# Local attention outputs from the third batch on: probabilities stationary, values moving, rows through DRAM into x by DMA transposes

## The chip, the cores and the metric

One core of a Trainium2 chip runs the whole kernel. The metric is the device time of one execution in microseconds (us), lower is better; the number for a kernel is the median of several executions. One further execution was taken with the hardware profiler, and every duration below comes from that one.

## What is computed

The reference is an attention with two fixed masks, followed by a bilinear feed-forward layer:

```python
# q, k, v: 8 batches, 8 heads, 576 positions, 64 features
rel = pos[:, None] - pos[None, :]
mask_local   = (rel >= 0) & (rel < 32)                                  # heads 0 to 3
mask_strided = (rel >= 0) & (pos[None, :] % 32 == pos[:, None] % 32)    # heads 4 to 7
attn = softmax(where(mask, q @ k.T / 8, -1e9));  o = attn @ v
x = o.transpose(0, 2, 1, 3).reshape(4608, 512)
out = ((x @ w_a) * (x @ w_b)) @ w_out       # w_a, w_b: 512 x 1536, w_out: 1536 x 512
```

Inputs and output are float32 in DRAM; the kernel calculates in bf16 with float32 sums.

## The kernel before, in words

**Two pipelines in one stream.** The feed-forward works on 9 tiles of 512 tokens. A tile `t` takes 16 slots, numbered `16t` to `16t+15`: 12 slots `ffn_ab` (one 128-wide piece of `d_ff` each: 4 matmuls with `w_a`, 4 with `w_b`, all 512 columns wide, written at L581; then a copy by ACT and a product by DVE), and 4 slots for the output. Tiles 2 to 8 (`FAST_Y`) take the output from seven half-size products (`y_plan`, and `y_tail` for the last tile) that are summed in a Strassen-like way; tiles 0 and 1 use `ffn_y` (L732).

The attention of batch `b` is cut into 8 units `u`, two for each pair of heads `c = u // 2`: units 0 to 3 are the local heads (3 blocks of 96 queries, each against 128 keys), units 4 to 7 the strided heads (4 blocks of 72). A step `S u` makes the scores on PE, `Exp` on ACT (L392) and the mask on DVE (L402), and leaves the probabilities in `p`, with keys on the partitions. A step `V u` multiplies them with the values. These steps are put between the slots by hand: `STEPS` for batches 1 and 2, `LATER` and `IN_Y` for the others, with positions counted from slot `16(b-1)`; `take(i)` runs those of slot `i`, and those of `i - 0.5` lie in the middle of the slot's matmuls. All five engines run in the order in which the program issues (a manual schedule); a tile framework adds the semaphores.

**The result x.** `xT` holds x transposed, 128 rows of features by 4 chunks (chunk `c` is the pair of heads `c`), in a ring of 4 batches. Tile `t` reads the end of batch `t-1` and the beginning of batch `t`, so batch `b` has to be in `xT` when slot `16b` starts. The first slot of a tile takes chunks 0, 1 and 2 first and chunk 3 last (for tile 1: chunk 1 last).

**The step V.** Two forms are in the kernel. For batches 0 and 1, `V_p` (L441) has the probabilities as weights (128 columns loaded) and 65 columns of values and ones moving; the result has queries on the partitions and the sum of the probabilities in column 65. `V_r` (L449) takes the reciprocal of the sums, `V_n` (L464) multiplies, and `step_X` (L510, L522) transposes on PE and copies into `xT`. From batch 2 on (`FIRST_D`), `step_VT` (L485) has the values as weights, with 64 columns of ones beside them, and 96 columns (strided: 72) of probabilities moving. The result is already transposed, and the sums stand in partitions 64 to 127. ACT makes the reciprocal as `Exp(-Ln(sum))` (L494, L495), and DVE multiplies straight into `xT`, one instruction for each head of the pair (L499 local, L501 strided).

**Loads.** K and Q of the batches from 2 on are loaded by GpSimd DMAs, transposed in blocks on DVE (`step_D`, L326 and L331), and put in place by DMAs on SP's queue (L341 for K, L345 for Q: ten for the local heads and ten for the strided heads of each batch). The local Q of batch `b` follows in slot `16(b-2)+9` (for batch 3: slot 27). The stores of the output stand on SP's queue too. SP issues in order, and in the built program each DMA also waits until the one eight places before it has landed.

**Tail.** `y_tail` makes the last tile's 14 products (seven kinds `k`, for even and odd rows `q`) in `TAIL_ORDER`. `y_post` moves each from PSUM (kinds 1, 7, 6, 5 and 3 by ACT, 4 and 2 by DVE; `+` is an addition on DVE), and `y_store` sends each finished part. The very last product, `21`, is made in two halves of 128 columns.

`fill_v` sets the columns of ones (64 to 127 of `vl` and `vs`) by GpSimd; `consts` has set column 64 alone already.

Of the kernel before, what the change touches and what calls it, by code (L numbers as in the profile page):

```python
# [8 lines left out]
BF16 = mybir.dt.bfloat16  # L9
# [5 lines left out]
FIRST_D = 2  # L15
RL = 6
RS = 8
# [4 lines left out]
LW = 96  # L22
# [8 lines left out]
def kernel(  # L31
# [10 lines left out]
    nc = tc.nc  # L42
    B, H, S, D = q.shape
# [9 lines left out]
    HL = H // 2  # L53
# [5 lines left out]
    sb = ctx.enter_context(tc.tile_pool(name="sb", bufs=3))  # L59
    fsb = ctx.enter_context(tc.tile_pool(name="ffn", bufs=2))  # L60
    pst = ctx.enter_context(tc.tile_pool(name="pst", bufs=1, space=bass.MemoryType.PSUM))
    dram = ctx.enter_context(tc.tile_pool(name="dram", bufs=2, space=bass.MemoryType.DRAM))
# [19 lines left out]
    vl_buf = [const.tile([128, HL * 6, VW], BF16, name=f"vl{i}") for i in range(2)]  # L82
# [30 lines left out]
    def zero_qz(i, eng, parts=((0, 0), (0, 1), (1, 0), (1, 1))):  # L113
        for j, z in parts:
            t = qz_buf[i][j][z]
            if (i, j, z) == (0, 0, 0):
                t = t[:, 1]
            if eng is nc.scalar:
                nc.scalar.copy(t, spare[:, :1].unsqueeze(2).to_broadcast(list(t.shape)))
            else:  # L120
                eng.memset(t, 0.0)
# [36 lines left out]
    XR = 4  # L158
    xT = const.tile([128, KD, XR * S], BF16)
# [11 lines left out]
    def fast_w(n, gs):  # L171
        a, b = ((wov[:, 0, 1], wov[:, 0, 0]), (wov[:, 1, 1], wf[:, 0]), (wov[:, 1, 1], wov[:, 0, 1]),
                (wov[:, 1, 0], wf[:, 1]))[n]
        nc.vector.tensor_tensor(wf[:, n, gs], a[:, gs], b[:, gs], op=ALU.subtract)
# [3 lines left out]
    def blocks(nm, z):  # L178
        z = int(z)
        return sb.tile([128, 2, (S, RS * GP)[z]], BF16, tag=f"t{nm}{z}", name=f"t{nm}{z}", bufs=1)  # L180
# [84 lines left out]
    def by_row(t):  # L265
        return t.rearrange("p (r h d) -> p h r d", h=2, d=D)

    def pair_up(nm, c):

        if (nm, c) == ("k", 1):  # L270
            t = shared[1][:96, -RL * 128:]
        else:
            t = blocks(*{"k0": "q0", "q0": "q1", "q1": "k0"}[f"{nm}{c}"])
            t = t.rearrange("p h n -> p (h n)")[:96, :RL * 128]
        nc.vector.tensor_copy(by_row(t), nats[1, nm, False][:, 2 * c:2 * c + 2])
        paired[1, nm, c] = t.rearrange("p (r m) -> p r m", r=RL)
# [85 lines left out]
    def unit(u):  # L362

        c, half = u // 2, u % 2
        return (c, half, 128, LW, 3) if c < 2 else (c, half, NP, NP, 4)
# [46 lines left out]
    xn = {}  # L412
# [33 lines left out]
    def V_r(b, u):  # L446
        c, half, M, n, G = unit(u)
        rc = sb.tile([128, 2, 4], F32, tag="rc", name="rc")
        nc.vector.reciprocal(rc[:n, :, :G].unsqueeze(3), held[b, "o", u][1])  # L449
        held[b, "rc", u] = rc  # L450

    def V_n(b, u):
        c, half, M, n, G = unit(u)
        ov, _ = held.pop((b, "o", u))
        rc = held.pop((b, "rc", u))
        if (b, c // 2) not in xn:
            x = sb.tile([128, RS * 4 * D], BF16, tag="xr", name="xr", bufs=2)
            xn[b, c // 2] = x[:n, :S // n * 4 * D].rearrange("p (g h d) -> p g h d", h=4, d=D)
        x = xn[b, c // 2][:, :, 2 * (c % 2):2 * (c % 2) + 2, :]
        if c < 2 or b >= FIRST_D:  # L460
            dst = x[:, G * half:G * half + G].rearrange("p g j d -> p j g d")
        else:
            dst = x[:, :, half, :].rearrange("p (g j) d -> p j g d", j=2)
        nc.vector.tensor_mul(dst, ov, rc[:n, :, :G].unsqueeze(3).to_broadcast([n, 2, G, D]))  # L464

    def step_V(b, u):
        if b >= FIRST_D:
            step_VT(b, u)
            return
        V_p(b, u)  # L470
        V_r(b, u)
        V_n(b, u)

    def step_VT(b, u):

# [48 lines left out]
    def step_X(b, c):  # L524
# [15 lines left out]
    STEPS = {1: {5.5: "Tk2", 6: "Tq2", 7: "S4 Tk3", 7.5: "S5", 8: "Tq3", 8.5: "V4", 9: "S6 V5 Pk0", 9.5: "S7 Pq0",  # L540
# [4 lines left out]
    LATER = {-1: "S0", 0: "S1", 1: "V0", 2: "S2", 3: "V1", 4: "S3", 5: "V2", 6: "S4", 7: "V3", 8: "S5", 9: "V4", 10: "S6",  # L545
             11: "V5"}
    IN_Y = {2: "S7", 6: "V6", 11: "V7"}
    FN = {"Tk": step_Tk, "Tq": step_Tq, "S": step_S, "V": step_V, "X": step_X, "W": lambda b, n: fast_w(n, slice(0, 3)),
          "s": S_px, "m": S_m, "L": lead_vl, "Pk": lambda b, c: pair_up("k", c), "Pq": lambda b, c: pair_up("q", c),
          "Z": lambda b, n: zero_qz(0, nc.vector, ((1, 1),)), "D": lambda b, n: step_D(FIRST_D, 0, "k", n)}  # L550

    def run(b, slot):
# [77 lines left out]
    def col(j):  # L630
        return slice(HN * j, HN * (j + 1))

    def y_store(eng, t, y, i, q, n=slice(0, d_model)):
        rows = out[TTOK * t:TTOK * (t + 1), n].rearrange("(a i s q) c -> a s i q c", i=2, s=8, q=2)
        eng.dma_start(out=rows[:, :, i, q], in_=y[i][:, q, n])
# [4 lines left out]
    def y_post(k, y, q, bank, n=slice(0, HN)):  # L640

        part = lambda i, j: y[i][:, q, HN * j:HN * (j + 1)]
        if k == "+":
            nc.vector.tensor_tensor(part(1, 1), part(1, 1), part(0, 1), op=ALU.add)
        elif k in "1765":
            nc.scalar.copy({"1": part(0, 0), "7": part(0, 1), "6": part(1, 0), "5": part(1, 1)}[k], bank)  # L646
        elif k == "4":
            nc.vector.tensor_tensor(part(1, 0), bank, part(1, 0), op=ALU.add)
        elif k == "2":
            nc.vector.tensor_tensor(y[0][:, q, n], bank, y[0][:, q, n], op=ALU.add)  # L650
        elif k == "3":
            nc.scalar.copy(part(0, 1), bank)

    Y_ORDER = [(x[0], int(x[1])) for x in "10 11 70 71 60 61 40 41 50 51 20 21 30 31".split()]
    TAIL_ORDER = [(x[0], int(x[1])) for x in "10 70 11 71 60 61 40 41 50 51 30 31 20 21".split()]

    def y_plan(t):

# [22 lines left out]
    def y_tail(t):  # L681

        plan, y = products(t), y_bufs()
        banks = [{x: mm_bank([128, HN]) for x in "ZXY"},
                 {"X": psum4["o"].tile([128, 2, 512], F32, tag="o", name="end")[:, 0, :HN],
                  "Z": pst.tile([128, 2, 512], F32, tag="st", name="end")[:, 0, :HN]}]
        for k, q in TAIL_ORDER:
            b, lhs, rhs = plan[k]
            cuts = [slice(0, HN)]
            if (q, k) == (1, "2"):  # L690
                cuts = [slice(0, 128), slice(128, HN)]
            for n in cuts:
                if (q, k) == (1, "2"):
                    bank = mm_bank([128, 128])
                else:
                    bank = banks[q][b]
                for g in range(FG):
                    nc.tensor.matmul(bank, lhsT=lhs(g, q), rhs=rhs(g)[:, n], start=g == 0 and k in "172",  # L698
                                     stop=g == FG - 1, skip_group_check=True)
                    if g < FG - 1:  # L700
                        yield y
                y_post(k, y, q, bank, n)
                if k == "5":
                    y_post("+", y, q, None)
                    y_store(nc.sync, t, y, 1, q)
                elif (q, k) == (0, "2"):
                    y_store(nc.sync, t, y, 0, q)
                elif (q, k) == (1, "3"):
                    y_store(nc.scalar, t, y, 0, q, col(1))
                elif (q, k) == (1, "2"):  # L710
                    y_store(nc.scalar if n.start == 0 else nc.sync, t, y, 0, q, n)
                yield y
# [48 lines left out]
    with tc.manual_schedule(engines={ENG.PE, ENG.SP, ENG.Pool, ENG.DVE, ENG.Activation}):  # L761
# [11 lines left out]
        for x, src in ((raw[0], k), (raw[1], q)):  # L773
            nc.sync.dma_start(out=x[:96].rearrange("p (h r d) -> p h r d", h=2, d=D),
                              in_=src[0, 0:2].rearrange("h (p r) d -> p h r d", r=RL))
# [16 lines left out]
        for nm in ORDER:  # L792
            if nm[0] == "*":
                spin(int(nm[1:]))
            elif nm == "C0":
                for x, cp, n in ((raw[0], nc.vector.tensor_copy, "k"), (raw[1], nc.scalar.copy, "q")):
                    t = nats[0, n, False][:, 0:2].rearrange("p h r d -> p (h r d)")
# [40 lines left out]
        for b in range(1, B):  # L838
            for pos, names in (STEPS.get(b) or {16 * (b - 1) + x: n for x, n in LATER.items()}).items():
                steps.setdefault(pos, []).append((b, names.split()))  # L840
# [6 lines left out]
        def do(i, fn, *args):  # L847
            at.setdefault(i, []).append(lambda: fn(*args))

        soon = {}  # L850
        for t in FAST_Y[:-1]:
            soon[16 * t + 10] = [lambda t=t: fast_s(t, 2, slice(4, 6))]
            soon[16 * t + 11] = [lambda t=t, n=n: fast_s(t, n, slice(4, 6)) for n in (0, 1)]
        do(0, fill_v, vl_buf[0])
        do(0, fill_v, vs_buf[0])
        for c in range(4):
            do(0, load_wo, c)
# [25 lines left out]
        for i, jz in ((2, (0, 0)), (3, (1, 0)), (0, (0, 1))):  # L883
            do(i, zero_qz, 0, nc.vector, (jz,))
        do(14, rezero, 1)
        do(27, fill_v, vl_buf[1])
        do(28, fill_v, vs_buf[1])
        for n, slot in enumerate((16, 16, 19, 20)):
            do(slot, fast_w, n, slice(3, 6))
# [50 lines left out]
```

## Time and profile before

| What | Value |
|---|---|
| Median of 3 runs | 328.97 us (328.81, 328.97, 331.59) |
| The profiled execution | 330.64 us, of which the program's span is 328.9 us |
| PE, busy share of the span | 322.3 us (98%) |
| DVE / ACT / POOL | 251.6 us (76%) / 210.2 us (64%) / 151.4 us (46%) |
| DMA engines, mean busy share | 90% or more in most slices up to 222 us, then falling |
| First matmul of tile 2 | at 94.28 us |

The span begins with the first instruction of the program; some 1.7 us of the profiled execution lie around it. "Busy" for PE means that some matmul was in the array; the ends of matmuls are modelled, so the distance between starts says more than a duration.

How to read the lines that follow. A group of instructions has its line, engine, operation, output and inputs, form and count, then "busy us, mean ns" and the idle time before. A timeline line has its start, its length, and how many instructions were merged into it (x6). SPq is the issuing of a DMA on SP's queue, and its length is that of the issuing, not of the transfer.

### The profile page before, as it was taken

How to read it: one execution, taken by the hardware profiler on the slowest of the kernel's cores; microseconds unless marked ns; L12 is line 12 of the kernel's file. 1: busy time of each engine (PE TensorE's matmuls, PEld its weight loads, DVE VectorE, ACT ScalarE, POOL GpSimd, SP SyncE). 2: the span in 40 equal slices, each digit the busy share in tenths (PEclk: the TensorE clock that was granted, in tenths of full speed). 3: DMA queues.
4: the chain of work that ended last, by engine and by line, in shares of the span. 5: the costliest groups of instructions: out<-in, count | busy, mean ns of one | idle time of the engine just before them, and what ended most of it. 6: DMA issues, size and time to landing. Idle time of an engine off the chain costs nothing.

```text
span 328.9 us, 7658 instructions
## 1 busy us (share of the span) xinstructions
PE 322.3 (98%) x2820; PEld 206.2 (63%) x2820; DVE 251.6 (76%) x529; ACT 210.2 (64%) x345; POOL 151.4 (46%) x280
## 2 busy tenths in 40 slices
PE   8899999999999999999999999999999999999994
PEld 6664555455555577557999885559555954584474
DVE  7747797888877998799879988898878745626642
ACT  6753766468778776877677767776777743323341
POOL 8845947689956644763565446634012001100000
PEclk9979999999999999999999999999999999999999
DMA  9999999799999599999799979797024040004004
GB/s 159 139 204 203 200 184 171 150 170 142 141 214 108 94 87 93 90 225 107 73 85 179 148 77 97 140 193 84 20 63 128 2 131 0 0 2 129 0 2 128
DMA packets 98725, 37.50 MB, mean 114 GB/s; under 512 B 76672, under 2 KB 95744, under 8 KB 98688
## 3 DMA queue, kind: packets, MB, share of 16 engines
q0 software_dynamic: 85968, 19.48, 63.8%
q1 hardware_dynamic: 12432, 17.34, 17.7%
q8 instruction: 22, 0.36, 0.5%
q10 hardware_dynamic: 288, 0.20, 0.2%
q14 instruction: 15, 0.12, 0.1%
HBM read 39.51 MB, written 9.44 MB: 149 GB/s over the span
## 4 chain that ended last, share of the span: by engine, by line
PE 93%; POOL 2%; DMA 2%; DVE 1%; ACT 0%; issue 0%; POOLq 0%
PE mm L581 55%; PE mm L669 17%; PE mm L732 6%; PE st L384 4%; PE o L485 4%; DMA tk<-in_v_dram 2%; PE mm L698 2%; PE ab L581 1%; POOL shared L196 1%; PE end L698 1%; PE o L441 1%; POOL vl L224 1%; PE tp L510 1%; PE tp L286 0%; PE tp L295 0%
## 5 line engine op out<-in xcount | busy, mean ns | idle before, releaser
L581 PE MATMUL mm<-xT,wa_sb 128*128 128x512 bf16 (+1 forms) x472 | 110.3, 357 | 0.0
L581 PE MATMUL mm<-xT,wb_sb 128*128 128x512 bf16 (+1 forms) x472 | 110.2, 357 | 0.0
L598 ACT COPY a_sb<-mm 128x512 f32<-128x512 f32 x106 | 62.1, 586 | 45.3 <-PE mm L581 44.5
L906 POOL CAST pace<-pf 1x1 f32<-1x1 bf16 x87 | 24.6, 283 | 113.6 <-DVE pf L601 109.8
L581 PEld LDWEIGHTS <-wb_sb 128*128 128x128 bf16 x480 | 46.6, 98 | 44.6 <-issue 1.1
L601 DVE TENSOR_TENSOR pf<-a_sb,mm 128x512 bf16<-128x512 f32 x84 | 57.1, 679 | 18.4 <-PE mm L581 14.2
L581 PEld LDWEIGHTS <-wa_sb 128*128 128x128 bf16 x480 | 42.7, 98 | 31.3
L392 ACT ACTIVATE p<-st 128x576 bf16<-128x576 f32 (+1 forms) x64 | 41.6, 650 | 6.7 <-PE st L384 6.1
L494 ACT ACTIVATE xr<-o 64x576 f32<-64x576 f32 x48 | 31.1, 648 | 22.6 <-PE o L485 22.3
L495 ACT ACTIVATE xr<-xr 64x576 f32<-64x576 f32 x48 | 32.8, 684 | 1.5
L499 DVE TENSOR_TENSOR xT<-o,xr 64x288 bf16<-64x288 f32 x48 | 21.6, 450 | 13.8 <-ACT xr L495 13.2
L501 DVE TENSOR_TENSOR xT<-o,xr 64x288 bf16<-64x288 f32 x48 | 21.4, 446 | 11.9 <-ACT xr L495 11.2
L669 PEld LDWEIGHTS <-ps 128*128 128x128 bf16 x288 | 27.9, 98 | 3.1
L646 ACT COPY y_sb<-mm 128x512 f32<-128x512 f32 (+1 forms) x28 | 15.6, 556 | 18.5 <-PE mm L669 13.0
L669 PE MATMUL mm<-wf,ps 128*128 128x256 bf16 x216 | 25.6, 273 | 0.0
L732 PE MATMUL mm<-wo_sb,pf 128*128 128x512 bf16 x96 | 23.4, 379 | 0.0
L242 POOL DMA_DIRECT2D vs<-in_v_dram x24 | 19.7, 820 | 4.9 <-PE mm L669 2.4
L669 PEld LDWEIGHTS <-pf 128*128 128x128 bf16 x216 | 20.3, 98 | 2.5 <-issue 0.2
L669 PE MATMUL mm<-wo_sb,pf 128*128 128x256 bf16 x144 | 18.5, 273 | 0.1
L211 POOL DMA_DIRECT2D ql<-in_q_dram x24 | 16.0, 666 | 5.0 <-DMA wo_sb<-in_moe_w_out_dram 3.8
L211 POOL DMA_DIRECT2D kl<-in_k_dram x24 | 16.0, 667 | 4.9 <-issue 3.2
L615 DVE TENSOR_TENSOR ps<-pf 128x512 bf16<-128x512 bf16 (+1 forms) x48 | 17.8, 380 | 0.5
(152 smaller groups left out, 471.3 us busy)
## 6 DMA issues: line engine op xcount, KB each, us to landing
out_dram<-y_sb SPq DMA_DIRECT2D x12, 512.0 KB, 4.9
out_dram<-y_sb SPq DMA_DIRECT2D x11, 256.0 KB, 3.0
vl<-in_v_dram POOLq DMA_DIRECT2D x6, 384.0 KB, 6.7
kl<-in_k_dram POOLq DMA_DIRECT2D x24, 72.0 KB, 3.2
ql<-in_q_dram POOLq DMA_DIRECT2D x24, 72.0 KB, 3.4
vs<-in_v_dram POOLq DMA_DIRECT2D x24, 72.0 KB, 3.8
wo_sb<-in_moe_w_out_dram POOLq DMA_DIRECT2D x4, 384.0 KB, 9.1
natk<-in_k_dram POOLq DMA_DIRECT2D x20, 72.0 KB, 3.2
```

What stands on the lines that cost most here:

```text
L211: nc.gpsimd.dma_start(out=t[32 * h:32 * h + 32], in_=src[b, h].rearrange("(i y) d -> y i d", y=32))
L392: nc.scalar.activation(p[:M, :, :W], st[:M, :, :W], ACT.Exp, scale=scale)
L494: nc.scalar.activation(r, sums, ACT.Ln)
L495: nc.scalar.activation(r, r, ACT.Exp, scale=-1.0)
L499: nc.vector.tensor_mul(dst[:, W * half:W * (half + 1)], o[:64, j, :W], r[:, j])
L501: nc.vector.tensor_mul(dst.rearrange("d (p r) -> d p r", r=RS)[:, :, G * half:G * (half + 1)], o[:64, j, :W].rearrange("d (g p) -> d p g", ...
L581: nc.tensor.matmul(ps_[:, c0:c0 + n], lhsT=w[:, kk, 128 * f:128 * (f + 1)], rhs=xT[:, kk, x0:x0 + n], start=(kk == first and c0 == 0), sto ...
L598: nc.scalar.copy(a_sb, ab[0])
L601: nc.vector.tensor_mul(pf[:, f, :].rearrange("p (i a s) -> p a i s", i=2, s=16), halves(a_sb), halves(ab[1]))
L669: nc.tensor.matmul(bank[b][:, q], lhsT=lhs(g, q), rhs=rhs(g), start=k in "172" and q == 0 and g == 0, stop=g == FG - 1, skip_group_check=True)
L732: nc.tensor.matmul(ybank[j], lhsT=pf[:, f, 128 * j:128 * (j + 1)], rhs=wo_sb[:, f], start=(f == 0), stop=(f == FD - 1))
L906: nc.gpsimd.tensor_copy(pace, done)
```

## The change

Units 0 to 3 of batches 2 to 7 (24 units) take the form with the probabilities as weights again: `V_p`, `V_r`, `V_n`, into a tile `xl` of which there is one. Once `V3` has filled it, `O0` writes it as rows to a DRAM tile (two of these), by one DMA on SP's queue: 96 partitions by 6 rows of 512 bytes. Then `I0` and `I1` read it back with two DMA transposes, also on SP's queue, 576 rows by 128 columns each, into chunks 0 and 1 of `xT`. For batch 2, `O0` stands in slot 26 and `I0 I1` in slot 28; for later batches in slots 7 and 9 after `16(b-1)`. Units 4 to 7 stay as they were. The fill of the ones beside the local values goes. The last tile's products come in another order, and two of its stores move.

```diff
         if (b, c // 2) not in xn:
-            x = sb.tile([128, RS * 4 * D], BF16, tag="xr", name="xr", bufs=2)
+            if b >= FIRST_D:
+                x = sb.tile([128, RL * 4 * D], BF16, tag="xl", name="xl", bufs=1)
+            else:
+                x = sb.tile([128, RS * 4 * D], BF16, tag="xr", name="xr", bufs=2)
...
     def step_V(b, u):
-        if b >= FIRST_D:
+        if b >= FIRST_D and u >= 4:
             step_VT(b, u)
             return
...
+    scratch = {}
+
+    def rows_out(b, _):
+
+        scratch[b] = dram.tile([S, HL * D], BF16, tag="xd", name="xd")
+        nc.sync.dma_start(out=scratch[b].rearrange("(g p) e -> p g e", p=LW),
+                          in_=xn.pop((b, 0)).rearrange("p g h d -> p g (h d)"))
+
+    def rows_in(b, c):
+
+        nc.sync.dma_start(out=xT[:, c, S * (b % XR):S * (b % XR + 1)], in_=scratch[b][:, 128 * c:128 * (c + 1)],
+                          transpose=True)
...
-             2: {20: "S0", 20.5: "S1", 21.5: "V0", 22: "S2", 23: "V1", 23.5: "S3", 24.5: "V2", 25: "S4", 26: "V3", 26.5: "S5",
-                 27.5: "V4", 28: "S6", 28.5: "V5", 29: "S7", 29.5: "V6", 30.5: "V7"}}
-    LATER = {-1: "S0", 0: "S1", 1: "V0", 2: "S2", 3: "V1", 4: "S3", 5: "V2", 6: "S4", 7: "V3", 8: "S5", 9: "V4", 10: "S6",
+             2: {20: "S0", 20.5: "S1", 21.5: "V0", 22: "S2", 23: "V1", 23.5: "S3", 24.5: "V2", 25: "S4", 26: "V3 O0", 26.5: "S5",
+                 27.5: "V4", 28: "S6 I0 I1", 28.5: "V5", 29: "S7", 29.5: "V6", 30.5: "V7"}}
+    LATER = {-1: "S0", 0: "S1", 1: "V0", 2: "S2", 3: "V1", 4: "S3", 5: "V2", 6: "S4", 7: "V3 O0", 8: "S5", 9: "V4 I0 I1", 10: "S6",
              11: "V5"}
...
-    TAIL_ORDER = [(x[0], int(x[1])) for x in "10 70 11 71 60 61 40 41 50 51 30 31 20 21".split()]
+    TAIL_ORDER = [(x[0], int(x[1])) for x in "10 70 60 11 40 50 71 30 61 20 51 41 31 21".split()]
...
                 if k == "5":
                     y_post("+", y, q, None)
+                if k == "54"[q]:
                     y_store(nc.sync, t, y, 1, q)
...
                 elif (q, k) == (1, "3"):
-                    y_store(nc.scalar, t, y, 0, q, col(1))
+                    y_store(nc.sync, t, y, 0, q, col(1))
...
-        do(0, fill_v, vl_buf[0])
         do(0, fill_v, vs_buf[0])
...
-        do(27, fill_v, vl_buf[1])
         do(28, fill_v, vs_buf[1])
```

More of the change, by code (lines that the diff above doesn't have):

```diff
@@ L548 @@
     FN = {"Tk": step_Tk, "Tq": step_Tq, "S": step_S, "V": step_V, "X": step_X, "W": lambda b, n: fast_w(n, slice(0, 3)),
-          "s": S_px, "m": S_m, "L": lead_vl, "Pk": lambda b, c: pair_up("k", c), "Pq": lambda b, c: pair_up("q", c),
+          "s": S_px, "m": S_m, "L": lead_vl, "O": rows_out, "I": rows_in, "Pk": lambda b, c: pair_up("k", c), "Pq": lambda b, c: pair_up("q", c),
           "Z": lambda b, n: zero_qz(0, nc.vector, ((1, 1),)), "D": lambda b, n: step_D(FIRST_D, 0, "k", n)}
```

## The prediction

> **What bounds the kernel.** I read the page first: the busy shares, the slices, the chain that ended last.
>
> ```profile
> PE 322.3 (98%) x2820; PEld 206.2 (63%) x2820; DVE 251.6 (76%) x529; ACT 210.2 (64%) x345; POOL 151.4 (46%) x280
> ...
> PEclk9979999999999999999999999999999999999999
> DMA  9999999799999599999799979797024040004004
> ...
> PE 93%; POOL 2%; DMA 2%; DVE 1%; ACT 0%; issue 0%; POOLq 0%
> ```
>
> PE is busy for all of the span but the ends, at the full granted clock from the fourth slice on, and 93% of the chain is PE. Busy alone proves little, so I compared the distances between matmul starts: those 512 wide stand 0.216 us apart throughout. After 22 us all gaps beyond such distances come to about 0.3 us. So an edit pays only by what it takes from PE's stream or from the tail, and every wait that reaches PE is paid in full. The DMA engines are 90% busy or more in most slices until 222 us.
>
> Next, the groups by shape, for what is exchanged:
>
> ```profile
> L495 ACT ACTIVATE xr<-xr 64x576 f32<-64x576 f32 x48 | 32.8, 684 | 1.5
> L494 ACT ACTIVATE xr<-o 64x576 f32<-64x576 f32 x48 | 31.1, 648 | 22.6 <-PE o L485 22.3
> ...
> L499 DVE TENSOR_TENSOR xT<-o,xr 64x288 bf16<-64x288 f32 x48 | 21.6, 450 | 13.8 <-ACT xr L495 13.2
> ...
> L485 PE MATMUL o<-p,vl 128*128 128x96 bf16 x144 | 10.0, 206 | 0.0
> ...
> L464 DVE TENSOR_TENSOR xr<-o,rc 96x384 bf16<-96x384 f32 x8 | 4.3, 547 | 0.2
> ...
> L441 PE MATMUL o<-vl,p 128*128 128x65 bf16 x48 | 2.6, 194 | 0.3 <-DMA vl<-in_v_dram 0.3
> ...
> L449 DVE RECIPROCAL rc<-o 96x6 f32<-96x6 f32 x8 | 1.5, 190 | 2.5 <-PE o L441 2.4
> ```
>
> The new form of a local unit runs here already, in batches 0 and 1 (L441, L449, L464), so it has prices. The durations of 206 and 194 ns hide the difference, since each includes the pipeline's end. The timeline of PE shows it, one unit of each form between its neighbours:
>
> ```profile
> 57.02 0.34 PE L441 MATMUL o<-vl,p 128*128 128x65 bf16 x6
> 57.20 0.60 PE L732 MATMUL mm<-wo_sb,pf 128*128 128x512 bf16 x2
> ```
>
> ```profile
> 200.56 0.42 PE L485 MATMUL o<-p,vl 128*128 128x96 bf16 x6
> 200.82 0.38 PE L581 MATMUL mm<-xT,wa_sb 128*128 128x512 bf16 x1
> ```
>
> From the unit's start to the next work's: 0.18 us with 65 columns moving, 0.255 us (unrounded) with 96.
>
> **PE's saving.** 24 units (6 batches by 4) times 0.075 us is 1.8 us, all of it on the path. Bounds: 1.7 to 1.9, the rounding of the two rows. Here a rule speaks against the change. The Trainium skill, "TensorE: Matmul & The Clock Gate", section "Back-to-back issue gap", has a sustained pair of weight load and matmul at about 81 ns for 128 columns, set by both; if the load of 128 weight columns set the pace, narrowing what moves would save nothing, and the sum would be 1.8 us worse. The rows disagree: the pairs stand 42.5 and 29.5 ns apart, in proportion to the columns.
>
> **ACT and DVE.** ACT loses 24 × (648 + 684) = 32 us. DVE exchanges 2 × 450 ns for 190 + 547 ns, 24 × 163 = 3.9 us less, and it no longer waits for ACT's two passes. I take nothing for either: the PE stream beside them has no stalls that a faster ACT or DVE could remove beyond the 0.3 us. The cover is PE's own work; it could be lost only if DVE became late, and it has less to do. The two fills on POOL (1.4 us each) go too, at nothing: POOL mostly waits for the pace of DVE.
>
> **The new path through SP.** O0 is a 288 KB write, I0 and I1 are 144 KB reads with transposition. I0 must wait until O0 has landed; for batches 3 to 7, SP's ten DMAs for the next batch's local Q and K are queued behind that wait, and S0 of the next batch, on PE, waits for those. The slack is long: the units V3 of batches 3 to 6 start at 109.89, 143.91, 178.10 and 212.46, the tiles that need them at 128.47, 162.50, 197.02 and 231.04, 18.6 to 18.9 us later. The chain between: 1.2 us on DVE; O0's issue and landing, at most 6.5 (the longest store's); two issues of 0.6; a landing of at most 5.9 (the longest on SP between 85 and 92 us): 14.8 us. SP is at its busiest for batch 6: two stores and two K blocks hold it until 216.3; then 6.5 + 1.2 + 5.9 ends at 229.9, still before 231.04. Next batch's Q: the DMAs that began at 220.03 there had landed for S0 by 224.46, and S0 starts at 230.5; with O0 landed at 219.3 (3 us) to 222.8 and two issues they begin 0.5 to 4 us later. Zero for all these; up to 1 us each if every bound meets.
>
> Batch 2 is different. There, Q of batch 3 goes to SP in slot 27, ahead of I0 and I1 in slot 28, and a store stands between:
>
> ```profile
> 85.14 0.54 SPq L345 DMA_DIRECT2D qz10l<-tq  x1
> ...
> 89.54 1.22 SPq L345 DMA_DIRECT2D qz11l<-tq  x1
> 90.80 0.60 SPq L345 DMA_DIRECT2D qz10l<-tq  x1
> 91.62 0.51 SPq L345 DMA_DIRECT2D qz11l<-tq  x1
> 92.23 1.50 SPq L743 DMA_DIRECT2D out_dram<-y_sb  x3
> ```
>
> ```profile
> 94.28 0.81 PE L581 MATMUL mm<-xT,wa_sb 128*128 128x512 bf16 x3
> ```
>
> The ten DMAs keep SP from 85.14 to 92.13, though the chunk that tile 2 takes first, at 94.28, now comes behind them. Worked forward: O0 goes out at about 82 (V3's matmuls at 79.85, reciprocal and product in DVE's order), before Q is ready, and has long landed. Batch 3's Q waits for a DVE transposition that ended at 85.11; in DVE's new order (each V 0.16 us shorter, no wait for Ln and Exp) I get 84.3. So the ten end between 90.6 (without the 1.22 us stall) and 92.1, the first store 0.6 later, I0 goes out between 91.2 and 92.8, I1 0.6 us after. I take I1 at 92.9. PE needs I1's chunk with tile 2's second matmul, at 94.50.
>
> How long a transposing DMA takes, no row shows. Nearest rows: on this queue from 85 us on, blocks of 36 to 40 KB land 1.8 to 5.9 us after issue, and the stores of 256 KB at 92 to 94 us in 2.3 to 3.5. I take 3.0, as the plain DMAs nearest in size and place. I1 then lands at 95.9, and PE stands for 1.4 us. Bounds: 91.8 + 1.8 = 93.6, no stall; 93.4 + 5.9 = 99.3, 4.8 us; with the 9.1 us that a 384 KB block of the third weight matrix takes on GpSimd's queue (the median there), 8.0 us.
>
> The skill has a price: "VectorE: DVE Perf Modes", section "The three transpose paths", gives 1309 ns for 128×128 through the DMA crossbar, which for 576 rows is 5.9 us in series (an estimate), 11.8 for both chunks, and would make the stall about 9 us and the time about 336; no row here shows it.
>
> **The tail.** The chain's end:
>
> ```profile
> 323.75 1.47 ACTq L635 DMA_DIRECT2D out_dram<-y_sb  x2
> 324.00 0.96 DVE L650 TENSOR_TENSOR y_sb<-mm,y_sb 128x256 f32<-128x256 f32 x3 [1.14 <-PE mm L698]
> 324.49 1.19 SPq L635 DMA_DIRECT2D out_dram<-y_sb  x2
> ```
>
> The last product is the same, so DVE ends at 324.97 as before. SP's last store went out at 325.12 because the one before it held SP until 325.03; in the new order that one (kind 3, ready after its copy at about 324.4) ends SP's issue at about the same time. What changes is traffic: the 256 KB of `20` leave some 2 us earlier, and 128 KB stand in front of the last 64 KB. Those took 2.72 us to land, the 128 KB store 2.52. I take 0.2 us gained; bounds −0.1 (PE may wait where `60` follows `10` with one product between; `30` after `50` does so before without a gap) and 0.4.
>
> **The sum.** The profiled execution took 330.64 us (span 328.9 and 1.7 around it): −1.8 − 0.2 + 1.4 is −0.6, or 330.0 on its scale. It lies 1.67 above the median, so on the median 328.97 − 0.6 = 328.4.
>
> **Rivals.** *In time:* I0 and I1 land by 94.5 (an SP queue without its 1.22 us stall, and a landing near 2.5 us). Then 328.97 − 2.0 = 327.0, between 326.7 and 327.4. For: DVE and ACT are relieved just there. Against: landings of 3.7 to 5.9 us on that queue between 85 and 90.
>
> *Slow transposes:* the crossing of a row-wise source into 128 partitions takes a good deal longer than a plain copy, or the SP queue spends more than 0.6 us to issue one. It decides at tile 2's first two matmuls, and makes the kernel slower by over 1% (332.3) from a stall of 5.3 us, I1 landing after 99.8. At 9.1 us from issue the stall is 7.5 and the time 334.5. A longer gap can also cost the clock: the page's slice with a clock of 7 is where matmuls of 512 stood twice as far apart after early gaps. For: nothing in the rows excludes it, and DMA engines are 90% busy there. Against: 256 KB stores land in 2.3 to 3.5.
>
> *No narrower in effect:* weight loads set the pace of the new units, PE saves nothing, 330.2 with the stall. The rows of batch 1 speak against it.
>
> **How the numbers follow.** Stall of 0.4 to 5.3 us at tile 2 (327.4 to 332.3): 0.39, forecast 328.4. In time: 0.24. Slow transposes: 0.28. No narrower: 0.03. A gain that I see no row for, below 325.7: 0.06. So faster by over 1% 0.06, within 1% 0.66, slower by over 1% 0.28; 1% is about what a measurement of this kernel can tell from no change. The range goes from 326.6, the lower end of "in time", to 334.5, leaving out half of "slow transposes" (0.14) and the 0.06 below.
>
> **What would show it.** In the profile after: the local units' starts 0.18 us apart from the next work; L494, L495 halved in count, L499 gone; the gap before tile 2's first or second matmul, near 94 us, against I0's and I1's landing; no gap at the starts of tiles 3 to 7, and none before S0 of batches 4 to 7; the last landing some 0.2 us sooner after PE's end. I am wrong if the landing of a transpose lies outside 1.8 to 5.9 us, if gaps appear at the later tiles (then SP's wait for O0, not batch 2's place in the queue, is what costs), or if PE's distances do not shrink.

## The result and the profile after

| | Before | After |
|---|---|---|
| Median | 328.99 us (4 executions, 328.81 to 331.59) | 333.0 us (4 executions, 332.53 to 334.68) |
| Ratio, 95% interval | | 1.0116, 1.0079 to 1.0153 |
| The profiled execution, its span | 330.64, 328.9 us | 334.68, 333.0 us |

The kernel became 4 us slower, where 0.6 us faster was forecast. A ratio leaves out executions that took over 1.5% more than the fastest of their kernel: in the experiments one of e2, three of e8, and one of the kernel before. First the page of the changed kernel, the lines that were shown of before:

```profile
PE 321.2 (96%) x2788; PEld 204.9 (62%) x2820; DVE 246.7 (74%) x529; ACT 178.8 (54%) x297; POOL 148.1 (44%) x278
...
PEclk9999999999978999999999999999999999999998
DMA  9999999999996897999999999999226030004004
...
PE 82%; DMA 5%; DVE 4%; POOL 3%; issue 2%; SPq 1%; ACT 1%; DVEq 0%; POOLq 0%
```

ACT's busy time fell by 31.4 us (32 had been worked out) and DVE's by 4.9 (3.9), and it bought nothing. (32 records of matmuls are missing from this trace: 2788 of 2820.) PE's share of the chain fell from 93% to 82%, and DMA's rose from 2% to 5%. The clock's row has a 7 and an 8 in the twelfth and thirteenth slices, from 91.6 to 108.2 us; before's 7 in the third slice, from 16 to 25 us, is gone. (The 8 in the last slice lies behind the last matmul.) So something happens around tile 2's start. The groups by shape and the timeline of PE say that the exchange itself came as planned:

```profile
L511 ACT ACTIVATE xr<-xr 64x576 f32<-64x576 f32 x24 | 16.4, 683 | 0.8
L510 ACT ACTIVATE xr<-o 64x576 f32<-64x576 f32 x24 | 15.6, 648 | 10.6 <-PE o L501 10.5
L467 DVE TENSOR_TENSOR xl<-o,rc 96x384 bf16<-96x384 f32 x24 | 13.3, 554 | 0.8
L441 PE MATMUL o<-vl,p 128*128 128x65 bf16 x192 | 10.9, 193 | 0.3
```

```profile
103.24 0.34 PE L441 MATMUL o<-vl,p 128*128 128x65 bf16 x6
103.42 0.81 PE L597 MATMUL mm<-xT,wa_sb 128*128 128x512 bf16 x3
```

A unit of the new form takes 0.18 us of PE's stream. Next, the timeline of PE where tile 2 begins (L597 is before's L581; brackets hold the idle time in front and what ended it):

```profile
95.96 0.59 PE L597 MATMUL mm<-xT,wa_sb 128*128 128x512 bf16 x1 [3.53 <-DMA xT<-xd]
97.32 0.59 PE L597 MATMUL mm<-xT,wa_sb 128*128 128x512 bf16 x1 [0.77 <-DMA xT<-xd]
98.12 1.49 PE L597 MATMUL mm<-xT,wb_sb 128*128 128x512 bf16 x3 [0.22 <-issue]
```

Without the wait the first of these matmuls would have begun at 92.27, right behind S0 of batch 3, and the second at 92.48. They began at 95.96 and 97.32, one for each transpose: a gap of 3.7 us and one of 1.1, together 4.8 by distances of starts. Then the clock, as busy times by stretch; the columns are the stretch, its length, PE's busy time (and matmuls), then PE's weight loads, DVE, ACT and POOL, and last the granted clock, the DMA share (the whole time of all packets begun in the stretch, so it can pass 1) and GB/s:

```profile
88.00:92.20 4.20, 4.20 (x32) 2.04 (x30) 2.19 (x4) 3.17 (x5) 1.91 (x4) 1.00 1.25 139
92.20:95.50 3.30, 0.23 (x6) 0.12 (x3) 2.07 (x4) 1.22 (x3) 1.49 (x3) 1.00 1.35 196
95.50:102.30 6.80, 5.35 (x17) 2.21 (x18) 1.32 (x3) 1.24 (x2) 0.42 (x2) 0.50 0.78 169
102.30:110.00 7.70, 7.65 (x56) 3.95 (x56) 6.03 (x12) 3.50 (x6) 5.35 (x11) 1.00 0.85 89
```

PE is idle in nearly all of the second stretch, and in the third, after the wait, it runs at half clock: the rows change at 95.47 and 102.29, two windows of 3.41 us, and matmuls of 512 columns start 0.43 us apart.

Why were the transposes late? The timeline of SP's queue, to be read against before's (there the ten DMAs for batch 3 began at 85.14 and S0 of batch 3 at 94.03; here at 83.36 and 92.01):

```profile
80.74 0.53 SPq L482 DMA_DIRECT2D xd<-xl  x1
83.36 0.54 SPq L345 DMA_DIRECT2D qz10l<-tq  x1
...
89.51 0.59 SPq L345 DMA_DIRECT2D qz11l<-tq  x1
91.41 0.35 SPq L760 DMA_DIRECT2D out_dram<-y_sb  x1
91.81 2.57 SPq L487 DMA_TRANSPOSE xT<-xd  x2
```

The rows were written early: O0 was issued at 80.74 and had landed by 85.45. SP then worked on the ten DMAs until 90.1, waited until 91.4, issued a store, and only then came to the two transposes. The chain of waits between 90 and 97 us (start, length, what) says what held SP:

```profile
85.22 6.58 DMA qz11l<-tq
91.80 0.02 issue
91.81 1.27 SPq L487
93.08 0.04 issue
93.13 4.15 DMA xT<-xd
```

I0 was let go at 91.80 by the landing of a 36 KB block that had been issued at 85.22, the eighth DMA before it; the store in front waited for its own eighth likewise. I0 landed at 95.92 (4.1 us), I1, issued 1.3 us later, at 97.28 (4.15 us).

Last, a table by stage: the first and the last stage boundaries are the span's ends, and those between are the first product on DVE of tiles 1, 3 and 8 (two kernels of the experiments beside them, in us):

| Stage | Before | After | e7 | e4 |
|---|---|---|---|---|
| start to tile 1 | 61.09 | 59.11 | 58.98 | 59.24 |
| tile 1 to tile 3 | 69.55 | 76.73 | 69.23 | 73.98 |
| tile 3 to tile 8 | 166.23 | 165.37 | 164.92 | 164.89 |
| tile 8 to the end | 32.07 | 31.76 | 31.79 | 31.77 |

The first row has none of the change in it: before's profiled execution ran at half clock from 18.30 to 21.71 us, which cost it 1.7 us (it lies 1.65 above its median), and after's did not. Leaving that out, the changed kernel's profiled execution lost 7.2 at tile 2 and gained 0.9 and 0.3 behind it. That is more than the 4.0 between the medians, and 334.68 is the highest of its four executions. The other three have no trace, but their granted clock is on record: 0.987 over the span for 334.68 and 333.27 us, 0.995 for 332.53 and 332.73. One window of 3.41 us at half clock lowers it by 0.005, so the half clock was shorter in the last two.

### The profile page after: what moved, and what is told of

Same layout as the page of the kernel before. It is cut to its first block, busy times and chain, and to the rows that moved or that the text cites. A ratio compares the mean times of both kernels' runs of the same rounds, so it can differ in the third digit from the quotient of the medians.

```text
span 333.0 us, 7577 instructions
## 1 busy us (share of the span) xinstructions
PE 321.2 (96%) x2788; PEld 204.9 (62%) x2820; DVE 246.7 (74%) x529; ACT 178.8 (54%) x297; POOL 148.1 (44%) x278
## 4 chain that ended last, share of the span: by engine, by line
PE 82%; DMA 5%; DVE 4%; POOL 3%; issue 2%; SPq 1%; ACT 1%; DVEq 0%; POOLq 0%
PE mm L597 49%; PE mm L685 14%; PE st L384 4%; PE mm L749 3%; PE o L441 3%; PE misc L154 2%; DMA qz11l<-tq 2%; PE mm L714 2%; DMA qz10l<-tq 1%; PE o L501 1%; DMA xT<-xd 1%; PE end L714 1%; PE ab L597 1%; SPq L345 1%; DMA natq<-in_q_dram 1%
## 5 line engine op out<-in xcount | busy, mean ns | idle before, releaser
L597 PE MATMUL mm<-xT,wa_sb 128*128 128x512 bf16 (+1 forms) x452 | 109.4, 360 | 5.1 <-DMA xT<-xd 4.3
L597 PE MATMUL mm<-xT,wb_sb 128*128 128x512 bf16 (+1 forms) x464 | 110.0, 359 | 0.6 <-issue 0.2
L617 DVE TENSOR_TENSOR pf<-a_sb,mm 128x512 bf16<-128x512 f32 x84 | 57.3, 682 | 33.8 <-PE mm L597 23.3
L921 POOL CAST pace<-pf 1x1 f32<-1x1 bf16 x87 | 23.5, 270 | 116.3 <-DVE pf L617 100.0
L597 PEld LDWEIGHTS <-wb_sb 128*128 128x128 bf16 x480 | 46.6, 98 | 44.9 <-issue 1.8
L597 PEld LDWEIGHTS <-wa_sb 128*128 128x128 bf16 x480 | 42.6, 98 | 36.6 <-issue 5.7
L517 DVE TENSOR_TENSOR xT<-o,xr 64x288 bf16<-64x288 f32 x48 | 21.4, 445 | 15.3 <-ACT xr L511 15.0
L510 ACT ACTIVATE xr<-o 64x576 f32<-64x576 f32 x24 | 15.6, 648 | 10.6 <-PE o L501 10.5
L619 DVE TENSOR_TENSOR pf<-a_sb,mm 128x512 bf16<-128x512 f32 x22 | 14.9, 676 | 4.9 <-ACT a_sb L614 2.7
L441 PEld LDWEIGHTS <-p 128*128 128x128 bf16 (+1 forms) x256 | 13.0, 97 | 7.7 <-DVE xr L467 1.1
```

What stands on the lines that cost most here:

```text
L441: nc.tensor.matmul(of[:, j, i, :w], lhsT=pt, rhs=vt, start=True, stop=True)
L517: nc.vector.tensor_mul(dst.rearrange("d (p r) -> d p r", r=RS)[:, :, G * half:G * (half + 1)], o[:64, j, :W].rearrange("d (g p) -> d p g", ...
L597: nc.tensor.matmul(ps_[:, c0:c0 + n], lhsT=w[:, kk, 128 * f:128 * (f + 1)], rhs=xT[:, kk, x0:x0 + n], start=(kk == first and c0 == 0), sto ...
L617: nc.vector.tensor_mul(pf[:, f, :].rearrange("p (i a s) -> p a i s", i=2, s=16), halves(a_sb), halves(ab[1]))
L921: nc.gpsimd.tensor_copy(pace, done)
```

## The experiments

The theory: the loss is all at tile 2's start, and comes from batch 2's place in SP's queue, with a late landing and the half clock behind the gap. Against it stood that the path through DRAM costs something at every batch, that the transposing itself is what is slow, and that the gain, where there is one, comes from ACT and DVE and not from PE's columns. Each ratio is against the kernel before on the same chip (medians 328.94 for the first four, 329.26 for the others).

**e1_rows_from_b3**: the change, but batch 2 in the old form.

```diff
-        if b >= FIRST_D and u >= 4:
+        if b >= FIRST_D and (u >= 4 or b == 2):
...
-  25: "S4", 26: "V3 O0", ... 28: "S6 I0 I1",
+  25: "S4", 26: "V3", ... 28: "S6",
...
+        do(0, fill_v, vl_buf[0])
```

> Batch 2 keeps values as weights and writes into x as before; batches 3 to 7 take the rows and the transposes. Theory (the loss is batch 2's late transposes alone: a gap of some 4.8 us at tile 2 and the half clock behind it): no gap near 94 us, no half clock after the start, 20 units by 0.075 us and 0.2 us of the tail saved: 329.0 - 1.7 = 327.3 us (326.8 to 327.8). Rival A (SP's waits and the added DMA traffic cost at every batch): five sixths of the loss stays, about 332. Rival B (narrower matmuls save nothing on PE): 328.8.

Measured: 327.75 us, ratio 0.9959 (0.9936 to 0.9982).

```profile
92.97 0.21 PE L384 MATMUL st<-qz11l,kT1l 128*128 128x96 bf16 x1
93.01 0.81 PE L597 MATMUL mm<-xT,wa_sb 128*128 128x512 bf16 x3
```

No gap stands at tile 2, and the clock is full there. Five batches through DRAM gain, so a cost at every batch that would make up the loss is ruled out.

**e2_rows_b2_only**: the opposite, batch 2 alone by rows (and the new tail).

```diff
-        if b >= FIRST_D and u >= 4:
+        if b >= FIRST_D and (u >= 4 or b > 2):
...
-    LATER = {... 7: "V3 O0", 8: "S5", 9: "V4 I0 I1",
+    LATER = {... 7: "V3", 8: "S5", 9: "V4",
...
+        do(0, fill_v, vl_buf[0])
+        do(27, fill_v, vl_buf[1])
```

> Rows and transposes for batch 2 alone; batches 3 to 7 as before the change; the tail's new order stays. Theory: the whole loss is here: 329.0 - 0.3 (4 units) - 0.2 (tail) + 4.8 (gap) + 1.7 to 3.4 (one or two windows at half clock) = 335.0 to 336.7 us, slower than the full change by about the 1.5 us that the other 20 units save. Rival A (a cost at every batch): a sixth of it, about 329.5.

Measured: 333.33 us (331.45 to 337.37), ratio 1.0100 (1.0049 to 1.0152).

```profile
95.96 0.21 PE L384 MATMUL st<-qz11l,kT1l 128*128 128x96 bf16 x1
99.76 1.44 PE L597 MATMUL mm<-xT,wa_sb 128*128 128x512 bf16 x3 [3.59 <-DMA xT<-xd]
```

A gap of 3.8 us stands at tile 2, with half clock from 99.65 to 103.06. The profiled execution is the one of 337.37, which also ran at half clock from 17.73 to 24.55, before anything that was changed; the other three took 331.45 to 333.91 us. Batch 2 alone makes a loss about as large as that of the whole change. It lies below what was expected, and the granted clocks of the three (0.999, 0.995 and 0.994) say that the half clock was short in them or did not come.

**e3_tail_only**: the kernel before with the new order of the tail and its two stores.

```diff
-    TAIL_ORDER = ... "10 70 11 71 60 61 40 41 50 51 30 31 20 21"
+    TAIL_ORDER = ... "10 70 60 11 40 50 71 30 61 20 51 41 31 21"
```

> The kernel before with the new order of the last tile and its two moved stores, nothing else. Theory: 0.2 us gained, 328.8 us (328.5 to 329.1), no gap between the last tile's products. Rival (a product waits for the copy of the one before it in the same bank, or SP's queue becomes the tail): 329.5 or more.

Measured: 328.71 us, ratio 0.9995 (0.9970 to 1.0019). By the traces, from the last matmul's start to the end of the span are 4.52 us before, 4.34 here, 4.21 in the changed kernel. The 0.2 are there in each trace; the times alone can't confirm them.

**e4_filler**: the changed kernel with 22 matmuls on weights, into a bank that nobody reads, ahead of tile 2's first matmul, so that PE waits at work.

```diff
+                if t == 2:
+                    spare_bank = mm_bank([128, TTOK])
+                    for _ in range(22):
+                        nc.tensor.matmul(spare_bank, lhsT=wa_sb[:, 0, :128], rhs=wa_sb[:, 0, :TTOK], start=True, stop=True)
```

> The changed kernel with 22 matmuls of 512 columns on weights alone, into a bank that nobody reads, put before tile 2's first matmul: they fill 4.75 us of the gap and keep PE at work. Theory: the gap's 4.8 us stay lost, the half clock behind it does not come: 333.0 less 1.7 to 3.4 = 329.6 to 331.3 us, granted clock 1.0 from 95 to 103 us. Rival C (half the clock costs nothing beyond the gap, or has another cause): 333 or more, with the half clock still there.

Measured: 332.34 us, ratio 1.0101 (1.0053 to 1.0149), above what was expected. The same stretch, and PE's timeline:

```profile
95.50:102.30 6.80, 6.80 (x43) 3.28 (x41) 2.98 (x7) 2.16 (x4) 1.88 (x5) 1.00 0.73 139
```

```profile
92.16 4.91 PE L610 MATMUL mm<-wa_sb 128*128 128x512 bf16 x22
96.90 0.81 PE L597 MATMUL mm<-xT,wa_sb 128*128 128x512 bf16 x3
```

The clock stays whole: 43 matmuls in 6.8 us, the filler's among them, where the changed kernel made 17. In the traces tile 1 to tile 3 is 2.8 us shorter than in the changed kernel. But here the transposes had landed by 95.35 and 95.70, so that the wait would have been some 3.2 us at the first matmul, and the filler kept PE until 96.90, 1.2 us longer than the wait. One trace with a shorter wait would prove little; but the granted clock was 0.999 or 1.000 in all four executions of e4, and 0.987 to 0.995 in all ten of the changed kernel (e11 included). So that the half clock comes from the idle gap is shown; how much of the changed kernel's median it makes is not, since the medians are only 0.5 to 0.7 us apart.

**e7_between**: batch 2's two transposes issued after the first four of the ten DMAs, so ahead of the other six and of the store.

```diff
+                if (b, z, nm, c) == (FIRST_D + 1, 0, "q", 0):
+                    rows_in(FIRST_D, 0)
+                    rows_in(FIRST_D, 1)
...
-  28: "S6 I0 I1",
+  28: "S6",
```

> The changed kernel with batch 2's two transposes issued earlier on the same queue: after the four DMAs of batch 3's Q that S0 of batch 3 needs (in slot 27), before the six of the second pair of heads and before the store. Theory (the place behind all ten and the store is the loss): I0 goes out near 86, I1 near 87.3, both landed by 91.5, no gap at tile 2, no half clock after the start: 329.0 - 2.0 = 327.0 us (326.6 to 327.6), some 0.3 below the kernel that leaves batch 2 as it was. Rival (the loss is the transposes' own slowness in loaded DMA engines): they land after 93, a gap of 1 us or more stays, 328 or more.

Measured: 327.40 us (326.63 to 327.97), ratio 0.9943 (0.9928 to 0.9959): faster than both kernels. SP's queue and then PE's timeline:

```profile
85.16 2.63 SPq L490 DMA_TRANSPOSE xT<-xd  x2
87.89 1.49 SPq L341 DMA_DIRECT2D kT1l<-tk  x2
```

```profile
91.86 0.21 PE L387 MATMUL st<-qz11l,kT1l 128*128 128x96 bf16 x1
91.90 0.59 PE L600 MATMUL mm<-xT,wa_sb 128*128 128x512 bf16 x2
92.55 0.81 PE L600 MATMUL mm<-xT,wb_sb 128*128 128x512 bf16 x3
```

No gap is left. The transposes took 5.8 and 5.0 us to land here, at 90.92 and 91.48; the second was 0.6 us ahead of its need at 92.1. Nothing but the place was changed, so the place is the cause. The granted clock was 0.998 or more in all six executions.

**e6_b2_ahead**: the transposes ahead of all ten.

```diff
-  27.5: "V4", 28: "S6 I0 I1",
+  27: "I0 I1", 27.5: "V4", 28: "S6",
```

> The changed kernel with batch 2's two transposes in slot 27, ahead of all ten DMAs for batch 3. Theory: SP waits there for the rows to land (85.4 in the changed kernel) and takes 2.5 us to issue the two; batch 3's first four DMAs start near 88 instead of 83.4 and land near 95 to 96 instead of 91.8, and S0 of batch 3, wanted at 92.0, waits for them: the gap moves from tile 2's first matmul to S0, 3 to 4 us, with a window at half clock: 331 to 333.5 us. Rival (any earlier place on the queue removes the loss): 327.0.

Measured: 329.15 us, ratio 1.0014 (0.9988 to 1.0041), better than the 331 to 333.5 us expected.

```profile
94.16 0.20 PE L384 MATMUL st<-qz10l,kT1l 128*128 128x96 bf16 x1 [1.37 <-DMA kT1l<-tk]
94.53 0.20 PE L384 MATMUL st<-qz11l,kT1l 128*128 128x96 bf16 x1 [0.16 <-DMA qz11l<-tq]
```

The gap did move to S0 of batch 3, whose Q and K now come late, but it is only some 1.9 us in all, in two pieces (1.5 and 0.3), and no half clock follows in this execution. (Three of the ten, 330.64 to 332.64 us, had a clock of 0.990 to 0.992; without a trace it can't be said where.) The order of these twelve DMAs decides who waits; e7's serves both.

**e5_b2_act**: batch 2's transposes on ACT's queue, at the same place in the program.

```diff
-        nc.sync.dma_start(
+        (nc.scalar if b == 2 else nc.sync).dma_start(
```

> The changed kernel with batch 2's two transposes issued from ACT's queue in slot 28 instead of SP's. Theory (SP's queue holds them up): they go out near 85.5 to 87 and land by 91.5, so no gap at tile 2; but ACT waits for the rows to land and spends 2.5 us issuing, the passes Ln and Exp of V5 come 2 to 3 us late, and V6 on PE waits for its bank: a gap of up to 2.7 us near 87 to 90. 327.0 to 330 us. Rival (the transposes land late wherever they are issued): a gap of over 2 us stays at tile 2's first matmul, 331 or more.

Measured: 330.92 us, ratio 1.0048 (1.0024 to 1.0072), above the 327 to 330 expected. ACT, then PE:

```profile
85.62 3.85 ACTq L487 DMA_TRANSPOSE xT<-xd  x2
89.52 0.65 ACT L510 ACTIVATE xr<-o 64x576 f32<-64x576 f32 x1 [4.68 <-issue]
```

```profile
91.97 0.57 PE L501 MATMUL o<-p,vs 72*128 72x72 bf16 x8 [3.73 <-DVE xT L517]
```

Tile 2, which begins at 98.31 here, finds its chunks, but issuing two transposes held ACT for 3.85 us; the strided unit's two passes behind them came late, then DVE's product, then V6 on PE, which waited for that product. The gap of 3.7 us was again followed by half clock, from 92.09 to 95.50, in this execution; by the granted clocks, half of the ten had none (see below). The transposes landed at 92.67 and 93.73, not by 91.5 as expected, so without the gap at V6 they would have come too late for tile 2. Another queue moves the wait, and does not remove it.

**e8_plain_reads**: the reads as plain DMAs of the same bytes. The local chunks of x are not transposed in it, for all six batches.

```diff
-        nc.sync.dma_start(out=xT[...], in_=scratch[b][:, 128 * c:128 * (c + 1)], transpose=True)
+        flat = scratch[b].rearrange("s e -> (s e)").rearrange("(p x) -> p x", p=128)
+        nc.sync.dma_start(out=xT[...], in_=flat[:, S * c:S * (c + 1)])
```

> The changed kernel with the twelve DMA transposes replaced by plain DMAs of the same bytes at the same places of the queue; the transposition of the local chunks is left out, so x is not the reference's. Theory (place first, the price of a transpose second): an issue of 0.5 to 0.6 us instead of 1.26, landings of 2.5 to 3.5 us instead of 4.1; I1 lands 1.3 to 2.3 us sooner, the gap at tile 2 shrinks from 4.8 to between 2.5 and 3.5 us, with a window at half clock or none: 329.5 to 332.2 us. Rival (the transposing itself is the loss): no gap, 327.0 us.

Measured: 332.23 us (ten executions, 328.66 to 334.03), ratio 1.0062 (1.0036 to 1.0089). The view of the DMA's line in the changed kernel, then in e8 (issuing in ns, then the time from issue to landing):

```profile
L487 SPq DMA_TRANSPOSE xT<-xd x12: 1138/1258/1486, 91.8 to 256.9; - x12
...
DMA to landing us min/median/max: 2.7/3.6/5.5
```

```profile
L488 SPq DMA_DIRECT2D xT<-xd x12: 325/396/851, 91.9 to 254.1; - x12
...
DMA to landing us min/median/max: 2.2/3.0/4.8
```

```profile
96.59 1.17 PE L597 MATMUL mm<-xT,wa_sb 128*128 128x512 bf16 x2 [4.07 <-DMA xT<-xd]
```

Plain reads leave a gap of 4.6 us too, where 2.5 to 3.5 were expected, with half clock from 96.76 to 100.17: at this place they took 4.7 and 4.85 us to land. Transposing costs 0.9 us of SP's time for each DMA and some 0.6 of landing in the median. It is not what made tile 2 late in the profiled execution. By the ratios, 1.0062 here against 1.0099 and 1.0116 for the changed kernel, plain reads may give back 1.2 to 1.8 us; the intervals overlap, so this is not shown. Most of the loss stays in either case.

**e9_96_columns**: e7 with 96 columns of values moving instead of 65; the columns beyond 65 are not read. (The two fills on POOL that set them to ones come back for it.)

```diff
+            E = 96 if b >= FIRST_D else D + 1
-                    vt = vl_buf[b % 2][:, ..., 0:D + 1]
+                    vt = vl_buf[b % 2][:, ..., 0:96 if b >= FIRST_D else D + 1]
```

> The kernel with batch 2's transposes between (no gap at tile 2), but with 96 columns moving instead of 65 in the local units of batches 2 to 7: 64 of values and 32 of ones, of which one is used. Theory (PE's time goes by the columns that move): the units take 0.255 us again instead of 0.18, 24 by 0.075 = 1.8 us more than that kernel, its ratio to the kernel before goes from 0.994 to 0.9995 (about 329.1 us). Rival B (weight loads set the pace): no more than that kernel, ratio 0.994 to 0.995.

Measured: 329.07 us, ratio 0.9995 (0.9967 to 1.0023), as expected; there is no gap at tile 2.

```profile
100.51 0.42 PE L445 MATMUL o<-vl,p 128*128 128x96 bf16 x6
100.77 1.03 PE L601 MATMUL mm<-xT,wa_sb 128*128 128x512 bf16 x4
```

The unit takes 0.26 us again, and e7's gain is gone, although ACT and DVE stay relieved. The weights loaded are the same 128 columns as in e7, so PE's time goes by what moves.

**e10_act_busy**: e7 with three passes of `Exp` over 390 columns on ACT behind each of the 24 local units, into a tile that is not read.

```diff
+            nc.scalar.activation(r, o[64:, :, :195], ACT.Exp)
+            nc.scalar.activation(r, r, ACT.Exp, scale=-1.0)
+            nc.scalar.activation(r, r, ACT.Exp, scale=-1.0)
```

> The same kernel with ACT given back about the time that the change takes from it: three passes of 390 columns, some 1.4 us, after each of the 24 local units, into a tile that nobody reads. Theory (ACT lies beside PE): nothing within 0.3 us, ratio 0.993 to 0.996. Rival (part of the gain is ACT's relief): 1 us or more slower than without the passes, ratio 0.997 or more.

Measured: 328.30 us, ratio 0.9972 (0.9946 to 0.9998). By the ratio this is on the rival's side (0.997 or more), though the interval reaches into what the theory expected. The trace says where: from tile 3 to tile 8, 16 local units, it takes 164.84 us, e7 164.92, so ACT's load costs nothing there. What the profiled execution took more than e7's, 1.9 us, is 0.6 before tile 1, where nothing was changed, and 1.4 between tiles 1 and 3.

```profile
94.06 0.59 PE L608 MATMUL mm<-xT,wa_sb 128*128 128x512 bf16 x2 [1.22 <-DMA xT<-xd]
```

Batch 2's second transpose landed at 94.02, and PE stood 1.4 us at tile 2's second matmul. Here O0 landed at 86.43 and I0 went out at 86.45, 1.3 us later than in e7. Whether ACT's passes made the rows late is not shown, so for batch 2 the rival stays open; the run does show how thin e7's margin of 0.6 us is.

**e11_change_again**: the changed kernel again, unedited, on the chip of e9 and e10.

> The changed kernel itself, beside the two others on the same chip: 332 to 333.5 us, ratio 1.010 to 1.015, gap of 4 to 5.5 us at tile 2's first three matmuls.

Measured: 332.86 us (332.26 to 334.08), ratio 1.0099 (1.0063 to 1.0134). Gaps of 3.75 and 0.88 us stand at tile 2, with half clock from 94.64 to 101.46. Gap and clock belong to the kernel. Here the half clock began within the gap, which lasts from 92.13 to 95.88; PE's row of stretches has 1.00 up to 94.60 and 0.50 from 94.70:

```profile
91.20:94.60 3.40, 1.09 (x10) 0.60 (x9) 2.07 (x4) 2.05 (x4) 2.10 (x5) 1.00 1.32 171
94.70:98.00 3.30, 1.61 (x4) 0.50 (x4) 0.00 (x0) 0.00 (x0) 0.00 (x0) 0.50 1.55 244
```

## Why the prediction was wrong

**PE's saving (1.8 us): right.** The distances are 0.18 and 0.255 us as the rows said. e7 takes 1.3 us less than before for the 16 units between tile 3 and tile 8, or 0.08 each. e9 takes the gain away by the columns alone, 1.67 us between its median and e7's. The loaded weights are 128 columns in both, and the pairs still stand 42.5 and 29.5 ns apart, in groups of six; so their load does not set the pace here, and "no narrower in effect" falls. The Trainium skill's 81 ns for a pair ("TensorE: Matmul & The Clock Gate", section "Back-to-back issue gap") are for 128 columns moving, a width that no pair of these units has.

**ACT and DVE (nothing): right as far as the runs tell.** e9 has both relieved, and its ratio to before is 0.9995 with an interval of 0.3% either way; e10's load on ACT costs nothing from tile 3 to tile 8. e10's whole time does not settle it for batch 2.

**The tail (0.2 us): right in size** by the traces, 0.2 to 0.3.

**SP's path for batches 3 to 7 (zero): right within its bound.** Their transposes landed 2.4 us or more before their tiles, and one gap is left, some 0.5 us before S0 of batch 7, where Q was late.

**Batch 2 (a stall of 1.4 us): here it failed**, at "I take I1 at 92.9" and at the landing of 3.0 behind it; the stall was 4.8. The path and the wait were the right ones, the sizes were not. Three terms were mis-sized, all to the same side. Against PE's need, I0 went out 1.5 us later than taken (0.46 us ahead of the first matmul's place instead of 2.0). DVE's relief did not start the ten DMAs earlier: they begin 8.65 us before S0 of batch 3, and 8.89 before the change, where I had 9.7 (94.03 less 84.3). And they, with the store, took 8.45 us instead of 8.0, since SP waited for the landing of the eighth DMA before. The second transpose came 0.7 us later than taken, because one holds SP for 1.26 us and not 0.6. Its landing took 4.15 and not 3.0, 1.15 more. 1.5 + 0.7 + 1.15 make the 3.4 us between 1.4 and 4.8. The sign of being wrong that the prediction named for the landings did not show: 2.7 to 5.5 us in the changed kernel lie inside 1.8 to 5.9.

**The clock: left out of the sum.** The prediction names it in the rival "slow transposes", and prices it nowhere. In the profiled execution tile 1 to tile 3 is 7.5 us longer than in e7; 4.8 are the gaps, so about 2.7 are the half clock, which is half of the 5.35 us that PE was busy in the two windows. Executions without a trace show it too: e5's ten fall into five with a granted clock of 0.999 or 1.000 (329.07 to 330.41 us) and five with 0.994 or 0.995 (331.43 to 332.95), 2.6 us apart in the median. At tile 2, the gaps in the traces that were followed by half clock are those of 3.5 us and more (the changed kernel twice, e2, e5, e8); behind the gaps of 1.5 us in e6 and 1.4 in e10 the clock stayed whole. The Trainium skill, "TensorE: Matmul & The Clock Gate", section "HAM oscillation — how this bites in real kernels", has the rule that there should be no idle gaps of more than about 3.4 us. The lengths of these gaps agree with it, but no run has one between 1.9 and 3.5 us; and in e11 the half clock began when PE had stood for 2.5 us, so 3.4 need not be over first. In the head the half clock came without such a gap (in before no gap in the 3.4 us ahead of it is longer than 0.6 us), and what brought it stays open.

So the time went where the rival "slow transposes" put it, but by another mechanism, and that 333.0 lies inside the stated range, which reaches up for that rival, is luck: the rival needed the transposing to be slow, and plain reads at that place are nearly as late (e8, 4.6 against 4.8 us). To be over 1% slower it needed a stall of 5.3 us, and the stall was 4.8; the rest came from the clock. Its second clause, an issue of more than 0.6 us, is true and makes 0.7 of the 4.8. "In time" (327.0) was the right forecast for the same edit with another order: e7, 1.9 us faster than before.

## What to carry to other kernels

A result that goes through a queue on its way is as late as its place in that queue: work back from the instruction that needs it, through the landing, the issue and what is queued in front, and where the margin is smaller than the spread of landings (2.5 to 7.1 us over the transposes of all these runs), move the place before anything else. On a stream that one engine fills, price a gap near 3.5 us with the half clock that may follow it, and read the granted clock of every execution, since the same kernel can come with it and without; one late transfer took back the saving of 24 units and 4 us more.

## What the runs showed of the hardware

- A transposing DMA of 144 KB holds SP's queue for 1.26 us in the median, a plain one for 0.40; on ACT two held it for 3.85. It lands nearly as fast as the plain one, 3.6 against 3.0 us in the median, and two in flight overlap. The 5.9 us in series that the prediction estimated from the Trainium skill ("VectorE: DVE Perf Modes", "The three transpose paths") is above nearly all of them; the longest seen are 7.1 and 6.7 (e5, the two on ACT's queue), 6.3 (e10) and 6.2 (e9).
- Blocks of 36 to 40 KB took 3.1 us to land in the changed kernel in the median, but up to 6.8 (a block of 36 KB, issued at 84.59), and the queue waited for them eight places later.
- The half clock came in windows of 3.41 us, one or two behind a gap, and also in the head of some profiled executions (one of before, at 18.3 us, two of e2), at some 1.7 us each, which is a difference between executions that has nothing to do with an edit.
